# One load per input and chunk, the odd heads' halves exchanged in the results, and a new written order in an RWKV-6 and mixture-of-depths kernel

## The chip, the cores and the metric

The kernel runs on one core of a Trainium2 chip. The metric is the device time of one execution in microseconds (us): the median of 3 runs was 328.4 us (327.49 to 330.77). Everything is float32, except a few selection matrices in bfloat16.

## The reference, cut to what matters

First an RWKV-6 attention with B = 4 sequences, H = 8 heads, S = 768 steps, D = 48 columns a head. Each head carries a 48x48 state over the steps:

```
cur      = (u * k[t]) outer v[t]
y[t]     = r[t] @ (state + cur)
state    = w[t][:, None] * state + k[t] outer v[t]
```

The results are put side by side to x of shape (4, 768, 384). Then mixture of depths, with F = 1024 and capacity 128:

```
scores = x @ w_gate
for b: top = the 128 rows of x[b] with the highest scores
       out[b] = x[b];  out[b, top] += sigmoid(scores) * (relu(x[b, top] @ w1) @ w2)
```

## The kernel before, in words

The steps are cut into chunks of 128 (`L`), six to a sequence, so 24 chunks `n` in all; a chunk has two halves `q` of 64 steps. Within a chunk the recurrence is turned into matrix products: `logs` takes ln w, `sums` adds it up along the steps with a triangular matrix on TensorE, and `falling` (exp of minus the sum) and `rising` (exp of the sum without the own step, which `exclusive` makes) give the factors `e` by which `scaled` multiplies k and r. `turned` transposes the scaled k and r on TensorE, `keep` copies them out of PSUM, `scores` multiplies them, `masked` takes the part under the diagonal (the diagonal itself, with u, comes from `own_products`, `own_weighted`, `own_sums` and `own_diagonal`). `kv` makes k times v for each half, `middle`, `after` and `carried` keep the state, `from_state` and `from_chunk` add up y in the PSUM tile `ps_y`, `results` copies it out, `store` writes it to `out`, and `scored` multiplies it with w_gate.

Heads stand in pairs (even, odd) in one array of 128 rows; an odd head has its two halves exchanged in the rows. In the kernel before that exchange happens in the load: each input of a chunk comes in three transfers (`load`, L125 for the even heads, L127 twice for the halves of the odd ones), and tiles are kept by type of head. The factors lie with the four pairs innermost, a step of four elements. The decay over a chunk is fetched as two rows of `e` by two small transfers on ScalarE's queue (`decay_rows`) and inverted on VectorE (`decay`). `in_range` sums how far w lies under 0.7; `tick` issues it and orders two groups of TensorE writes behind each other. At the end a flag made from `guard` decides whether a general, slow path is run.

The mixture of depths follows per sequence b: `spread`, `spread_kept` and `compare` compare each score with all earlier ones, `column_sums`, `ranks`, `picks`, `numbers` and `index` make the list of rows, `fetch` gathers them from `out` by an indirect transfer on GpSimd's queue, `fetched_turned` and `fetched_kept` transpose them, eight `first` and eight `second` steps are the two products (`hidden` is the relu between them), `mixed` adds, `put` scatters the rows back. I call the 16 steps of one sequence its products.

The order in which steps are issued is written by hand: `at(turn, offset, step, n)` gives each step a place, the list is sorted by it, and each engine works through its instructions in that order. All loads and stores go through SyncE's queue (SP) in the same order. Inputs have 10 buffers, x has 4, the PSUM tile `ps_s` serves the sums, the scores and (as `ps_x`) everything of the mixture but the two products, which use `ps_m`.

Of the kernel before, what the change touches and what calls it, by code (L numbers as in the profile page):

```python
# [40 lines left out]
def kernel(  # L41
# [30 lines left out]
    assert B * NCH < 256  # L72
# [18 lines left out]
    def at(turn, offset, f, *args):  # L91
        plan.append((turn * TURN + offset, len(plan), f, args))
# [10 lines left out]
    def source(x, b, ci, t, q=None):  # L103
        lo, n = ci * L, L
        if q is not None:
            lo, n = ci * L + (1 - q) * Q, Q
        return by_type_h(x[b])[:, t, lo:lo + n, :].rearrange("j s d -> s j d")

    def by_type_h(x):
        return x.rearrange("(j t) s d -> j t s d", t=2)  # L110

    def load(n, which):
        if n >= N:
            return
# [10 lines left out]
        nc.sync.dma_start(out=dst[:, 0], in_=source(x, b, ci, 0))  # L125
        for q in (0, 1):
            nc.sync.dma_start(out=dst[q * Q:(q + 1) * Q, 1], in_=source(x, b, ci, 1, q))  # L127
# [4 lines left out]
    upper = consts.tile([L, 2, L], FP32)  # L132
# [5 lines left out]
    junk_1 = consts.tile([L, 1], FP32)  # L138
# [4 lines left out]
    u_bc = consts.tile([L, 2, HP, D], FP32)  # L143
# [53 lines left out]
    def load_w1(i):  # L197
        nc.sync.dma_start(out=w1[:, i], in_=w1_src[:, i])
# [8 lines left out]
    def flat(t):  # L207
        return t.rearrange("p t j d -> p (t j d)")

    def logs(n):  # L210
        lw = get(n, "lw", lev, [L, 2, HP, D], bufs=3)
        nc.scalar.activation(out=flat(lw), in_=flat(T[n, "w"]), func=AF.Ln)  # L212

    def in_range(n):
        junk = lev.tile([L, C], FP32, tag="junk", name="junk", bufs=1)
        return nc.scalar.activation(  # L216
            out=junk, in_=flat(T[n, "w"]), func=AF.Relu, bias=low, scale=-1.0,
            accum_out=guard[:, 0, n:n + 1],
        )

    def sums(n):
        for t in (0, 1):
            nc.tensor.matmul(  # L223
                ps_s[:, 0, t * HP * D:(t + 1) * HP * D], upper[:, t], T[n, "lw"][:, t],
                start=(t == 0), stop=True, skip_group_check=True,
            )

    summed = ps_s[:, 0, 0:C]

    def falling(n):  # L230
        e = get(n, "e", lev, [L, 2, 2, D, HP])
        nc.scalar.activation(  # L232
            out=e[:, 0].rearrange("p t d j -> p t j d"),
            in_=summed.rearrange("p (t j d) -> p t j d", t=2, j=HP), func=AF.Exp, scale=-1.0,
            accum_out=guard[:, 1, n:n + 1],
        )

    def exclusive(n):
        ex = get(n, "ex", lev, [L, 2, HP, D])
        nc.vector.tensor_sub(flat(ex), summed, flat(T[n, "lw"]))  # L240

    def rising(n):
        nc.scalar.activation(  # L243
            out=T[n, "e"][:, 1].rearrange("p t d j -> p t j d"), in_=T[n, "ex"], func=AF.Exp,
            accum_out=guard[:, 2, n:n + 1],
        )

    def decay_rows(n):
        if chunks[n][1] == NCH - 1:
            return  # L250
        for t in (0, 1):
            p = L - 1 if t == 0 else Q - 1
            nc.scalar.dma_start(
                out=a_rows[n % 3][t * DP:t * DP + D, :], in_=T[n, "e"][p:p + 1, 0, t],
            )

    def decay(n):
        if chunks[n][1] == NCH - 1:
            return
        a = get(n, "a", lev, [L, HP])  # L260
        nc.vector.reciprocal(out=a, in_=a_rows[n % 3])

    def scaled(n):
        nc.vector.tensor_mul(  # L264
            kr_t[n % 2][:, :, :, :, 0:D].rearrange("p j i t d -> p (i t) j d"),
            T[n, "kr"].rearrange("p i t j d -> p (i t) j d"),
            T[n, "e"].rearrange("p i t d j -> p (i t) j d"),
        )

    def turned(n, i):  # L270
        for j in range(HP):
            nc.tensor.transpose(  # L272
                ps_k[:, i, j * L:(j + 1) * L], kr_t[n % 2][:, j, i].rearrange("p t d -> p (t d)"), ident
            )
# [21 lines left out]

    halves = [slice(0, Q), slice(Q, L)]
# [11 lines left out]
    def masked(n):  # L309
        sc = T[n, "sc"].rearrange("p (t j) s -> p t (j s)", t=2)  # L310
        nc.vector.copy_predicated(  # L311
            out=T[n, "sc"].rearrange("p (t j) s -> p t j s", t=2),
            mask=_heads(within, 2, HP),
            data=ps_s[:, :, 0:HP * Q].rearrange("p t (j s) -> p t j s", j=HP),
        )

    def kv(n):
        ci = chunks[n][1]
        if ci == NCH - 1:
            qs = ((0, 0), (1, 1))  # L320
        else:
            qs = ((0, 0), (1, 0), (0, 1), (1, 1))
        for j in range(HP):
            for t, q in qs:
                half = q ^ t
                nc.tensor.matmul(
                    ps_k[halves[t], half, j * D:(j + 1) * D],
                    kr_t[n % 2][halves[q], j, 0, t, :], T[n, "v"][halves[q], t, j, :],
                    start=(j == 0), stop=True, skip_group_check=True,
                )  # L330
# [12 lines left out]
    def after(n):  # L343
# [3 lines left out]
        T[n, "sum"] = s  # L347
        nc.vector.tensor_add(s, kv_of(1), T[n, "mid"])

    def carried(n):  # L350
        if chunks[n][1] == NCH - 1:
            return
        nc.vector.tensor_mul(T[n, "sum"], T[n, "sum"], T[n, "a"].to_broadcast([L, HP, D]))

    def waits(later, first):
        tc.add_manual_dep(
            later.ins, first.ins.name,
            mybir.DependencyInfo(mybir.DependencyClass.Sync, mybir.DependencyReason.DATA),
            reason="other rows of the array write the same results",
        )  # L360

    def tick(n):

        if n + 4 < N:
            i = in_range(n + 4)
        else:
            i = nc.scalar.copy(out=junk_1, in_=low)
        if n >= 0:
            waits(i, T[n, "behind"])
            T[n, "tick"] = i  # L370

    def from_state(n):
        ci = chunks[n][1]
        for j in range(HP):
            for half in (0, 1):
                if half == 0 and ci == 0:
                    continue
                s = T[n, "mid"] if half else T[n, "state"]
                for t in (0, 1):
                    q = half ^ t  # L380
                    T[n, "behind"] = nc.tensor.matmul(  # L381
                        ps_y[halves[half], t, j * D:(j + 1) * D],
# [4 lines left out]
    def from_chunk(n):  # L387
        ci = chunks[n][1]
        sc = T[n, "sc"].rearrange("p (t j) s -> p t j s", t=2)
        for j in range(HP):  # L390
            for t in (0, 1):
                for q in (0, 1):
                    half = q ^ t
                    m = nc.tensor.matmul(  # L394
                        ps_y[halves[half], t, j * D:(j + 1) * D],
                        sc[halves[q], t, j, :], T[n, "v"][halves[q], t, j, :],
                        start=(ci == 0 and half == 0 and j == 0), stop=True, skip_group_check=True,
                    )
                    if j == 0 and t == 0 and q == 0:
# [364 lines left out]
```

## Time and profile before

| | |
|---|---|
| median of 3 runs | 328.4 us (327.49 to 330.77) |
| the profiled execution | 327.58 us, of which the profile's span is 325.8 us |
| busy: TensorE (PE), VectorE (DVE), ScalarE (ACT), GpSimd (POOL) | 194.3, 144.9, 120.5, 90.0 us |
| first and last `results` copy | 42.11 us and 293.29 us |
| mean granted TensorE clock | 0.781 |

A row of a list over time gives the start in us, the duration in us, the engine (PEld is the weight load of TensorE, SPq the SyncE queue), the line, the operation, output and input, and, in brackets, how long the engine was idle before it and what ended that. Grouped rows give the busy time in us and the mean of one in ns. A table by stretches gives the busy time of PE, PEld, DVE, ACT and POOL, then the granted clock, the busy share of the 16 DMA engines and GB/s. In the 40 slices of the span a digit is a tenth.

### The profile page before, as it was taken

The page shows a single profiled execution, that of the slowest core. Times are in us where ns is not written, and L with a number is a line of the kernel's source. Part 1 is how long each engine was busy: PE and PEld are TensorE (multiplying, and loading weights), DVE is VectorE, ACT ScalarE, POOL GpSimd, SP SyncE. Part 2 cuts the span into 40 slices and gives each one's busy share as a digit, 9 for nine tenths or more (in the row PEclk, how much of TensorE's full clock was granted, in tenths as well). Part 3 has the DMA queues.
Part 4 walks back from the last instruction along what each step waited for, and adds up shares of the span by engine and source line. Part 5 has one row for each costly group of instructions (what it writes and reads, how often), then busy time and mean ns, then how long its engine had stood idle before and what let it go on. Part 6 is the DMA issues. An engine that isn't in the chain of part 4 may idle for free.

```text
span 325.8 us, 8831 instructions
## 1 busy us (share of the span) xinstructions
PE 194.3 (60%) x3634; PEld 161.0 (49%) x3634; DVE 144.9 (44%) x356; ACT 120.5 (37%) x285; POOL 90.0 (28%) x94
## 2 busy tenths in 40 slices
PE   2033577766004668005797875788787798784890
PEld 1033466555003557005686653577665587662860
DVE  2125335554002674006555675466567576634100
ACT  2305444454002454001655542666555445330100
POOL 3131332134003140016134442333444612312001
PEclk9999955587555675555989995899999659998596
DMA  4575675666666656567555555640000200001001
GB/s 77 101 127 102 141 157 112 115 138 137 134 143 121 119 109 117 113 121 143 110 110 91 110 111 123 146 84 27 27 26 26 74 26 26 26 27 50 24 0 35
DMA packets 112208, 29.40 MB, mean 90 GB/s; under 512 B 107168, under 2 KB 111392, under 8 KB 112160
## 3 DMA queue, kind: packets, MB, share of 16 engines
q1 hardware_dynamic: 109088, 27.15, 40.9%
q0 software_dynamic: 512, 1.57, 1.6%
q8 instruction: 30, 0.49, 0.7%
q10 hardware_dynamic: 2560, 0.03, 0.4%
q14 instruction: 18, 0.15, 0.1%
HBM read 23.20 MB, written 5.51 MB: 88 GB/s over the span
## 4 chain that ended last, share of the span: by engine, by line
PE 25%; SPq 21%; issue 10%; DVE 9%; ACT 9%; DMA 7%; POOL 1%; ACTq 1%; DVEq 0%; POOLq 0%
SPq L127 14%; PE ps_k L272 7%; SPq L125 6%; PE ps_m L544 5%; ACT e L232 3%; PE ps_m L558 3%; PE ps_y L394 2%; PE ps_s L223 2%; DVE ex L240 2%; DMA out_dram<-x 2%; DVE scr L424 2%; DMA a_row<-e 2%; ACT x L409 1%; PE ps_y L381 1%; PE ps_s L303 1%
## 5 line engine op out<-in xcount | busy, mean ns | idle before, releaser
L295 POOL TENSOR_TENSOR sc<-diag,own 128x512 f32<-128x512 f32 x24 | 31.5, 1313 | 140.6 <-DVE own L289 127.5
L272 PE MATMUL ps_k<-ident,kr_t 128*128 128x128 f32 x192 | 36.9, 355 | 17.6 <-DVE kr_t L264 9.9
L264 DVE TENSOR_TENSOR kr_t<-kr,e 128x768 f32<-128x768 f32 x24 | 37.2, 1549 | 18.1 <-ACT e L243 11.0
L240 DVE TENSOR_TENSOR ex<-ps_s,lw 128x384 f32<-128x384 f32 x24 | 13.4, 558 | 65.8 <-ACT e L232 65.8
L272 PEld LDWEIGHTS ps_k<-ident,kr_t 128*128 128x128 f32 x192 | 29.6, 183 | 22.8 <-issue 12.5
L223 PE MATMUL ps_s<-lw,upper 128*128 128x192 f32 x96 | 28.1, 433 | 6.0 <-ACT lw L212 6.0
L544 PE MATMUL ps_m<-xeT,w 128*128 128x128 f32 x192 | 29.9, 312 | 2.3 <-ACT xeT L515 2.3
L394 PE MATMUL ps_y<-v,sc 64*64 64x48 f32 x768 | 19.7, 249 | 18.1 <-ACT junk L216 16.8
L424 DVE CUSTOM_DVE_ANT_0 scr<-x,wg_bc 128x384 f32<-128x384 f32 x24 | 13.5, 561 | 37.5 <-ACT x L409 37.4
L544 PEld LDWEIGHTS ps_m<-xeT,w 128*128 128x128 f32 x192 | 27.7, 222 | 4.0 <-ACT xeT L515 3.7
L435 PE MATMUL ps_s<-ident,score 128*128 128x128 f32 x24 | 8.7, 363 | 34.5 <-DVE score L424 34.1
L409 ACT COPY x<-ps_y 128x384 f32<-128x384 f32 x24 | 11.5, 478 | 46.1 <-PE ps_y L394 24.4
L285 POOL TENSOR_TENSOR rk<-rk,u_bc 128x384 f32<-128x384 f32 x24 | 24.3, 1012 | 13.4 <-DMA u_bc<-in_u_dram 11.6
L243 ACT ACTIVATE e<-ex 128x384 f32<-128x384 f32 x24 | 21.9, 913 | 15.1 <-DVE ex L240 15.1
L303 PE MATMUL ps_s<-RT,KT 64*64 64x64 f32 x768 | 19.7, 247 | 13.0 <-DVE ex L240 13.0
L216 ACT ACTIVATE junk<-w,low 128x384 f32<-128x384 f32 x24 | 14.7, 614 | 34.3 <-DMA w<-in_w_dram 22.0
L394 PEld LDWEIGHTS ps_y<-v,sc 64*64 64x64 f32 x768 | 17.2, 162 | 20.3 <-issue 19.2
L278 ACT COPY KT<-ps_k 128x512 f32<-128x512 f32 x24 | 14.0, 584 | 34.7 <-PE ps_k L272 34.7
L311 DVE COPY_PREDICATED sc<-within,ps_s 128x512 f32<-128x512 uint32 x24 | 17.4, 724 | 20.5 <-POOL sc L295 18.2
L282 POOL TENSOR_TENSOR rk<-kr 128x384 f32<-128x384 f32 x24 | 24.1, 1004 | 5.3 <-DMA kr<-in_r_dram 5.3
L558 PE MATMUL ps_m<-w,hid 128*128 128x384 f32 x64 | 25.4, 512 | 0.0
L223 PEld LDWEIGHTS ps_s<-lw,upper 128*128 128x128 f32 x96 | 22.3, 268 | 6.0 <-ACT lw L212 6.0
(87 smaller groups left out, 317.3 us busy)
## 6 DMA issues: line engine op xcount, KB each, us to landing
out_dram<-x SPq DMA_DIRECT2D x24, 192.0 KB, 2.1
w<-in_w_dram SPq DMA_DIRECT2D x24, 96.0 KB, 2.6
w<-in_w_dram SPq DMA_DIRECT2D x48, 48.0 KB, 2.8
kr<-in_k_dram SPq DMA_DIRECT2D x24, 96.0 KB, 2.8
kr<-in_k_dram SPq DMA_DIRECT2D x48, 48.0 KB, 2.4
kr<-in_r_dram SPq DMA_DIRECT2D x24, 96.0 KB, 2.6
kr<-in_r_dram SPq DMA_DIRECT2D x48, 48.0 KB, 2.4
v<-in_v_dram SPq DMA_DIRECT2D x24, 96.0 KB, 2.7
```

Of the source, the lines that this page charges most:

```text
L127: nc.sync.dma_start(out=dst[q * Q:(q + 1) * Q, 1], in_=source(x, b, ci, 1, q))
L223: nc.tensor.matmul(ps_s[:, 0, t * HP * D:(t + 1) * HP * D], upper[:, t], T[n, "lw"][:, t], start=(t == 0), stop=True, skip_group_check=True,)
L243: nc.scalar.activation(out=T[n, "e"][:, 1].rearrange("p t d j -> p t j d"), in_=T[n, "ex"], func=AF.Exp, accum_out=guard[:, 2, n:n + 1],)
L264: nc.vector.tensor_mul(kr_t[n % 2][:, :, :, :, 0:D].rearrange("p j i t d -> p (i t) j d"), T[n, "kr"].rearrange("p i t j d -> p (i t) j d" ...
L272: nc.tensor.transpose(ps_k[:, i, j * L:(j + 1) * L], kr_t[n % 2][:, j, i].rearrange("p t d -> p (t d)"), ident)
L282: nc.gpsimd.tensor_mul(flat(rk), flat(T[n, "kr"][:, 0]), flat(T[n, "kr"][:, 1]))
L285: nc.gpsimd.tensor_mul(flat(T[n, "rk"]), flat(T[n, "rk"]), flat(u_bc))
L295: nc.gpsimd.tensor_mul(sc, _heads(diag, H), T[n, "own"].to_broadcast([L, H, Q]))
L303: nc.tensor.matmul(ps_s[halves[q], t, j * Q:(j + 1) * Q], T[n, "KT"][halves[t], j, halves[q]], T[n, "RT"][halves[t], j, halves[q]], start= ...
L394: m = nc.tensor.matmul(ps_y[halves[half], t, j * D:(j + 1) * D], sc[halves[q], t, j, :], T[n, "v"][halves[q], t, j, :], start=(ci == 0 and ...
L544: nc.tensor.matmul(p[:, (f % GF) * L:(f % GF + 1) * L], w1[:, dc, f * L:(f + 1) * L], T[b, "xeT"][:, dc, :], start=(dc == 0), stop=(dc == ...
L558: nc.tensor.matmul(ps_m[0][:, 0:C], T[b, "hid"][:, f, :], w2[:, f, :], start=(f == 0), stop=(f == NFC - 1))
```

## The change

- **Loads.** One transfer for each input and chunk, all eight heads in their own order, 128 rows; w of two chunks lies in one tile `ww`. So 96 transfers where there were 288. u comes in one transfer instead of two, and w1 in four pieces instead of three.
- **Exchange.** The halves of odd heads are exchanged when `results` copies y out of PSUM: one copy for the even heads (128 rows) and two for the odd ones (64 rows each). `sums` is one product with one triangular matrix.
- **Unstrided factors.** `e` has the layout of k and r; `falling` and `rising` write densely and no longer accumulate into `guard`.
- **One decay row.** A third exponential on ScalarE (`whole`, 32 rows, written with a step of four) takes the place of the inverse; one transfer on SP's queue (`decay_row`) spreads its last row to 128 rows of `a_all`.
- **Range check.** `in_range` runs once for two chunks; `tick` and its waits go, `masked` waits for `from_state` of its chunk instead.
- **PSUM.** The sums have a bank of their own (`ps_x`), spread and counts lie in the free columns of `ps_s`, the two products use one bank `ps_m`, and for the last sequence `ps_s` and `ps_y`. x has 8 buffers, the small tiles of the mixture one for each sequence.
- **Order.** Each step has a place in a table instead of a hand-written offset, with a turn of 5.6 instead of 6.

```diff
 def load(n, which):
...
-    nc.sync.dma_start(out=dst[:, 0], in_=source(x, b, ci, 0))
-    for q in (0, 1):
-        nc.sync.dma_start(out=dst[q * Q:(q + 1) * Q, 1], in_=source(x, b, ci, 1, q))
+    nc.sync.dma_start(
+        out=dst.rearrange("p (h d) -> p h d", d=D),
+        in_=x[b, :, ci * L:(ci + 1) * L, :].rearrange("h s d -> s h d"),
+    )
...
 def sums(n):
-    for t in (0, 1):
-        nc.tensor.matmul(
-            ps_s[:, 0, t * HP * D:(t + 1) * HP * D], upper[:, t], T[n, "lw"][:, t],
-            start=(t == 0), stop=True, skip_group_check=True,
-        )
+    nc.tensor.matmul(summed, upper, T[n, "lw"], start=True, stop=True)
...
+def falling(n):
+    e = get(n, "e", lev, [L, 2, C])
+    nc.scalar.activation(out=e[:, 0], in_=summed, func=AF.Exp, scale=-1.0)
...
+def whole(n):
+    nc.scalar.activation(
+        out=falls[n % 2][:, :, 0:D, :].rearrange("p t d j -> p j t d"),
+        in_=summed[L - 32:L].rearrange("p (j t d) -> p j t d", t=2, d=D), func=AF.Exp,
+    )
+def decay_row(n):
+    nc.sync.dma_start(out=a_all[:, n, :], in_=falls[n % 2][31:32].rearrange("p t d j -> p (t d) j"))
 def scaled(n):
     nc.vector.tensor_mul(
-        kr_t[n % 2][:, :, :, :, 0:D].rearrange("p j i t d -> p (i t) j d"),
-        T[n, "kr"].rearrange("p i t j d -> p (i t) j d"),
-        T[n, "e"].rearrange("p i t d j -> p (i t) j d"),
+        kr_t[n % 2][:, :, :, 0:D].rearrange("p i h d -> p (i h) d"),
+        T[n, "kr"].rearrange("p i (h d) -> p (i h) d", d=D),
+        T[n, "e"].rearrange("p i (h d) -> p (i h) d", d=D),
     )
...
+def results(n, i):
+    if i == 0:
+        get(n, "x", lev, [L, H, D], bufs=8)
+    t, to, of = ((0, slice(0, L), slice(0, L)), (1, halves[0], halves[1]),
+                 (1, halves[1], halves[0]))[i]
+    nc.scalar.copy(
+        out=T[n, "x"].rearrange("p (j t) d -> p t j d", t=2)[to, t],
+        in_=ps_y[of, t, 0:HP * D].rearrange("p (j d) -> p j d", d=D),
+    )
...
+TURN = 5.6
+CHUNK_PLACES = {
+    "logs": -13.529, "in_range": 5.037, "sums": -10.782, "falling": -9.639, "exclusive":
+    -8.766, "rising": -7.796, "whole": -7.379, "decay_row": -1.446, "scaled": -6.003,
+    "own_products": -8.375, "own_weighted": -3.602, "own_sums": -3.578, "own_diagonal":
+    -0.431, "turned0": -5.178, "turned1": -4.856, "keep0": -3.586, "keep1": -3.296, "kv":
+    -2.911, "middle": -1.837, "after": -0.334, "carried": 3.13, "from_state": -0.146,
+    "scores": -1.822, "masked": 0.287, "from_chunk": 1.759, "results0": 2.506, "results1":
+    2.801, "results2": 3.124, "scored": 4.614, "store": 15.942, "spread": 5.503,
+    "spread_kept": 6.774, "compare": 6.875, "load_w": -17.786, "load_k": -13.524,
+    "load_r": -14.443, "load_v": -7.489,
+}
...
+BATCH_PLACES = {   # one place for each of the four sequences
...
+    "first0": (26.258, 30.275, 87.674, 215.849),
...
+    "second3": (51.842, 70.51, 224.53, 411.339),
...
+    "mixed": (61.705, 86.818, 305.931, 496.549),
```

Chunk n stands at 5.6 n plus its place, sequence b at 5.6 (6 b + 5) plus its place. Sorted, the order within a turn m is:

```
PE:   sums m+1, turned m, from_chunk m-1, kv m, scores m, from_state m, spread m-1, sums m+2
ACT:  keep m, results m-1 (three), logs m+2, rising m+1, whole m+1, in_range, spread_kept m-1, falling m+2
DVE:  exclusive m+1, carried m-1, middle m, scored m-1, scaled m+1, after m, masked m, compare m-1, own_sums m+1
SP:   decay_row m+1, load w m+4, store m-2, load r m+4, load k m+4, load v m+3
```

The stores of chunks 12 to 17 stand about one turn later than this.

More of the change, by code (lines that the diff above doesn't have):

```diff
@@ L22 @@
 LOW = 0.7
-LIMIT = 1.0e30
+LIMIT = 1.0e15
 NIN = 10
-TURN = 6.0
 def _rows(ap, n):
@@ L197, in load_w1 @@
     def load_w1(i):
-        nc.sync.dma_start(out=w1[:, i], in_=w1_src[:, i])
+        part = slice(i * F // 4, (i + 1) * F // 4)
+        nc.sync.dma_start(out=w1[:, :, part], in_=w1_src[:, :, part])
     def load_w2(i):
@@ L315, in masked @@
         )
-    def kv(n):
[L318 to L322, printed above, removed]
-        for j in range(HP):
[L324 to L330, printed above, removed]
+        tc.add_manual_dep(
+            i.ins, T[n, "behind"].ins.name,
+            mybir.DependencyInfo(mybir.DependencyClass.Sync, mybir.DependencyReason.DATA),
+            reason="other rows of the array write the same results behind this",
+        )
+    def kv(n):
+        last = chunks[n][1] == NCH - 1
+        for j in range(HP):
+            for q in (0,) if last else (0, 1):
+                for t in (0, 1):
+                    nc.tensor.matmul(
+                        ps_k[halves[t], q, j * D:(j + 1) * D],
+                        kr_t[n % 2][halves[q], 0, 2 * j + t, :], T[n, "v"][halves[q], 2 * j + t, :],
+                        start=(j == 0), stop=True, skip_group_check=True,
+                    )
     def kv_of(half):
@@ L352, in carried @@
             return
[L353 to L370, printed above, removed]
+        s = T[n + 1, "state"]
+        nc.vector.tensor_mul(s, s, a_all[:, n, :].to_broadcast([L, HP, D]))
     def from_state(n):
@@ L434, in spread @@
     def spread(b, c):
-        nc.tensor.transpose(ps_x[:, 0:L], score[:, b, c:c + 1].to_broadcast([L, L]), ident)
+        nc.tensor.transpose(ps_row, score[:, b, c:c + 1].to_broadcast([L, L]), ident)
     def spread_kept(b, c):
@@ L539, with bank @@
     GF = 4
+    def bank(b, g):
+        return (ps_s[:, g] if g < 2 else ps_y[:, 0]) if b == B - 1 else ps_m
     def first(b, f):
-        p = ps_m[(f // GF) % 2]
+        p = bank(b, f // GF)
         for dc in range(NDC):
@@ new lines, in in_range_even @@
+    def in_range_even(n):
+        if n % 2 == 1:
+            in_range(n - 1)
+    STEPS = dict(
+        logs=logs, in_range=in_range_even, sums=sums, falling=falling, exclusive=exclusive,
+        rising=rising, whole=whole, decay_row=decay_row, scaled=scaled, own_products=own_products,
+        own_weighted=own_weighted, own_sums=own_sums, own_diagonal=own_diagonal,
+        turned0=lambda n: turned(n, 0), turned1=lambda n: turned(n, 1),
+        keep0=lambda n: keep(n, 0), keep1=lambda n: keep(n, 1), kv=kv, middle=middle, after=after,
+        carried=carried, from_state=from_state, scores=scores, masked=masked,
+        from_chunk=from_chunk, results0=lambda n: results(n, 0), results1=lambda n: results(n, 1),
+        results2=lambda n: results(n, 2), scored=scored, store=store,
+        spread=lambda n: spread(*chunks[n]), spread_kept=lambda n: spread_kept(*chunks[n]),
+        compare=lambda n: compare(*chunks[n]), load_w=lambda n: load(n, "w"),
+        load_k=lambda n: load(n, "k"), load_r=lambda n: load(n, "r"), load_v=lambda n: load(n, "v"),
+    )
```

330 lines of the change are left out of this document (124 added, 206 removed), and 10 rows, old and new, of the table BATCH_PLACES.

## The prediction

> **What bounds the kernel now.** I read the page first: busy shares, slices, the chain of work that ended last.
>
> ```profile
> span 325.8 us, 8831 instructions
> PEclk9999955587555675555989995899999659998596
> DMA  4575675666666656567555555640000200001001
> q1 hardware_dynamic: 109088, 27.15, 40.9%
> PE 25%; SPq 21%; issue 10%; DVE 9%; ACT 9%; DMA 7%; POOL 1%; ACTq 1%; DVEq 0%; POOLq 0%
> SPq L127 14%; PE ps_k L272 7%; SPq L125 6%; PE ps_m L544 5%; ACT e L232 3%; PE ps_m L558 3%; PE ps_y L394 2%; PE ps_s L223 2%; DVE ex L240 2%; DMA out_dram<-x 2%; DVE scr L424 2%; DMA a_row<-e 2%; ACT x L409 1%; PE ps_y L381 1%; PE ps_s L303 1%
> ```
>
> No engine is busy all the time. The chain runs to 20% through the issue of loads on SP's queue (L127, L125), and the DMA engines are about 60% busy until slice 27 (some 215 us), then nearly idle. So there are two stages, and the queue's own list of instructions shows the first.
>
> ```profile
> 8.52 0.60 SPq L125 DMA_DIRECT2D w<-in_w_dram  x1
> 9.17 1.25 SPq L127 DMA_DIRECT2D w<-in_w_dram  x2
> 32.57 2.38 SPq L127 DMA_DIRECT2D v<-in_v_dram  x2
> 98.94 0.55 SPq L413 DMA_DIRECT2D out_dram<-x  x1
> 107.22 0.55 SPq L413 DMA_DIRECT2D out_dram<-x  x1
> 216.09 78.04 SPq L413 DMA_DIRECT2D out_dram<-x  x11
> ```
>
> One issue takes 0.60 us and 0.65 with its gap, for 96 KB (L125) as for 48 KB (L127: 1.25 for two). A chunk has twelve loads and a store, and the stores of neighbours stand 107.22 - 98.94 = 8.28 us apart: that is the queue's pace until 216 us. The first store waits behind ten chunks of loads until 98.94. What that does is seen in the copies of y out of PSUM (L409), one a chunk:
>
> ```profile
> 42.11 0.48 ACT L409 COPY x<-ps_y 128x384 f32<-128x384 f32 x1 [1.31 <-PE ps_y L394]
> 71.13 0.48 ACT L409 COPY x<-ps_y 128x384 f32<-128x384 f32 x1 [0.88 <-PE ps_y L394]
> 101.19 0.48 ACT L409 COPY x<-ps_y 128x384 f32<-128x384 f32 x1 [21.64 <-DMA out_dram<-x]
> 145.48 1.21 POOL L502 DMA_INDIRECT xe<-out_dram,idx  x1 [27.51 <-DMA w<-in_w_dram]
> 210.19 0.48 ACT L409 COPY x<-ps_y 128x384 f32<-128x384 f32 x1 [0.88 <-PE ps_y L394]
> 252.37 0.48 ACT L409 COPY x<-ps_y 128x384 f32<-128x384 f32 x1 [0.88 <-PE ps_y L394]
> 293.29 0.48 ACT L409 COPY x<-ps_y 128x384 f32<-128x384 f32 x1 [0.88 <-PE ps_y L394]
> ```
>
> Chunk 0 comes at 42.11. Chunk 4 waits 21.6 us for a buffer of x that the late store holds; the first gather (L502) waits 27.5 us, until the last store of its sequence has landed, also late in SP's queue. In the second stage nothing waits for loads, and still five chunks, 13 to 18, take 252.37 - 210.19 = 42.2 us, 8.4 each. So the time is 42.1 (head) + 251.2 (23 steps, two with a stall) + 32.5 (tail) = 325.8.
>
> **The change, part by part.** SP's queue: per chunk four loads, a store and the decay row, 6 x 0.65 = 3.9 us, if one issue of all eight heads costs what the two sizes seen cost. Twice the packets of L125 were never issued at once, so bounds: 0.6 (no dependence, which the equal rows say) to 1.95 us (the three it replaces). I take 0.65. The Trainium skill, Perfetto Trace Analysis, What "DMA-bound" means, reads a solid row of issues as the generation of descriptors, so the cost would grow with packets; the equal 0.60 speaks against it here, and a rival below carries it.
>
> The transfers themselves stay, packet for packet, but for the small decay rows. Queue q1 took 40.9% of 325.8 = 133 us of all 16 engines, 5.55 us a chunk with stores and weights. The fullest 5 us show what share they reach:
>
> ```profile
> 20.00:25.00 5.00, 0.77 (x3) 1.00 0.86 153
> 206.00:293.00 87.00, 69.86 (x1570) 58.13 (x1566) 54.98 (x138) 44.20 (x107) 30.59 (x28) 0.92 0.16 43
> 210.00:252.40 42.40, 34.12 (x770) 27.85 (x762) 28.54 (x69) 24.91 (x60) 16.95 (x15) 1.00 0.16 40
> ```
>
> At 0.86 a chunk takes 5.55 / 0.86 = **6.45 us** (at 1.0, 5.55).
>
> Engines: the third row holds five chunks, so 6.8 us of PE, 5.7 of DVE and 5.0 of ACT each. These rows carry the edits:
>
> ```profile
> L264 DVE TENSOR_TENSOR kr_t<-kr,e 128x768 f32<-128x768 f32 x24 | 37.2, 1549 | 18.1 <-ACT e L243 11.0 <-DMA kr<-in_k_dram 2.0 <-DMA kr<-in_r_dram 1.9
> L447 DVE SCALAR_TENSOR_TENSOR ahead<-every,score,ahead_of 128x768 bf16<-128x768 f32 x4 | 4.0, 1011 | 0.7 <-ACT every L440 0.7
> L232 ACT ACTIVATE e<-ps_s 128x384 f32<-128x384 f32 x24 | 21.0, 874 | 2.0 <-PE ps_s L223 1.9
> L243 ACT ACTIVATE e<-ex 128x384 f32<-128x384 f32 x24 | 21.9, 913 | 15.1 <-DVE ex L240 15.1
> L212 ACT ACTIVATE lw<-w 128x384 f32<-128x384 f32 x24 | 12.6, 523 | 0.0
> L409 ACT COPY x<-ps_y 128x384 f32<-128x384 f32 x24 | 11.5, 478 | 46.1 <-PE ps_y L394 24.4 <-DMA out_dram<-x 21.6
> L440 ACT COPY every<-ps_s 128x128 f32<-128x128 f32 x24 | 6.4, 265 | 19.0 <-PE ps_s L435 18.7
> L278 ACT COPY KT<-ps_k 128x512 f32<-128x512 f32 x24 | 14.0, 584 | 34.7 <-PE ps_k L272 34.7
> ```
>
> - `scaled` on dense factors: between nothing gained (1.55) and the other fp32 operation of 768 elements (1.01). I take 1.0: DVE about 5.1 us a chunk, without the inverse less still.
> - `falling` and `rising`, dense and without reading an accumulator: as `logs`, 0.52 each, where 0.87 and 0.91 stood (at worst these). `whole` has the strided row's 0.87. `results`: three copies of 192 elements, between 0.265 (128) and 0.478 (384), so about 0.33 each, 1.0 in all for 0.48. The range check halves its fixed part. ACT stays near 5 us a chunk.
>
> PE loses the second triangular product's instructions; POOL does what it did. Now the loop. In the sorted order `turned` of a chunk stands behind `sums` of the next but one (they share `ps_x` with `whole`), so at full clock:
>
> ```profile
> 171.58 1.09 PE L272 MATMUL ps_k<-ident,kr_t 128*128 128x128 f32 x8 [0.34 <-DVE state L348]
> 172.51 0.82 PE L223 MATMUL ps_s<-lw,upper 128*128 128x192 f32 x4
> 43.91 1.97 PE L272 MATMUL ps_k<-ident,kr_t 128*128 128x128 f32 x8 [0.19 <-DVE state L348]
> 42.10:62.50 20.40, 15.65 (x282) 13.28 (x282) 10.26 (x24) 9.44 (x22) 6.14 (x6) 0.50 0.64 138
> ```
>
> `turned` 1.09, two `keep` 1.17, three `results` 1.0, `logs` 0.52, `rising` 0.52, `whole` 0.87, `sums` about 0.7, less some 0.1 of overlap at each of five ACT neighbours: 5.4 us around. A new wait in it is `sums` behind `whole`, and behind `sums` all of PE is queued; the other, `masked` behind `from_state`, ends well before DVE gets there. The decay row's wait holds SP's next loads, but those are wanted a turn or more later. So per turn: SP 3.9, loop 5.4, DVE 5.1, DMA 6.45. PE: 25 of the 64 product steps stand in the main loop, the rest behind it, about 0.7 us each:
>
> ```profile
> 214.27 1.34 PE ps_m L544 x12
> 298.56 3.18 DMA xe<-out_dram,idx
> 303.31 8.39 PE ps_m L544 x48
> 311.70 5.18 PE ps_m L558 x16
> 317.87 0.99 POOL out_dram L570
> ```
>
> (x12 are two `first` steps in 1.34; x16 are eight `second` in 5.18.) The stretch of five chunks held about one sequence's 16 steps, 10.6 us, so a bare chunk is (34.1 - 10.6) / 5 = 4.7, and the new main loop has 4.7 + 25 x 0.67 / 23 = 5.4. The transfers end last: I take **6.5 us** a turn.
>
> Head: `results` of chunk 0 stands behind `turned` of chunk 1, which needs w of chunk 2 by way of ACT's order. Ahead of that load SP has ten, 2.2 MB with one piece of w1; at 153 GB/s of the fullest window 14 us, plus 3 to issue and land, one load more (1.3), then `logs`, `rising`, `scaled`, `turned` and `from_chunk`, 4 us: **22**. Bounds 19 (larger packets move faster) and 27.
>
> Tail, from the last `results`: half of the products stand here. On PE five `second` of sequence 1 (3.2), all of sequence 2 and of sequence 3 (2 x 10.6), and some 6 for turns, counts and the one bank that sequence 2 has: 30.5; the gather's 3.2 us lie beside sequence 2. Behind PE come `mixed`, `put` and the end, 325.8 - 316.9 = 8.9 as before (PE ended at 311.70 + 5.18). **39**, against 32.5.
>
> Sum: 22 + 23 x 6.5 + 39 = 210.5; the profiled execution lay 1.8 over its span (327.58) and the median another 0.8 over that: **213 us**.
>
> **The rivals.**
>
> 1. *Engines bound, transfers fill up to 1.0.* 20 + 23 x 5.6 + 39 + 2 = 190. For it: 5.55 us of transfers fit. Against: no window is over 0.86.
> 2. *The pace stays.* Engines in order wait for each other as in chunks 13 to 18 (8.4), or the DMA share stays at 0.64 (5.55 / 0.64 = 8.7): 22 + 23 x 8.5 + 39 + 2 = 258. For it: both were measured. Against: the 8.4 had the strided operations and a decay row on ACT's queue inside the loop, and 0.64 went with a queue that issued no faster.
> 3. *The change's loads do not get cheaper to issue* (the skill's reading): 1.95 each, 4 x 1.95 + 1.2 = 9.0 a turn: 270.
> 4. *TensorE stays at half clock.* In 42.1 to 62.5 PE was busy 7.8 us a chunk at 0.50; `turned` took 1.97 for 1.09. With the products 1.3 more, 9.1 a turn, and 17 more in the tail: 289. For it: the slices show it at half for long stretches, 40 to 65 us among them. Against: with PE at 80% it was 1.00 for 42 us. The Trainium skill, TensorE: Matmul & The Clock Gate, PE-mode transpose, says that transposes don't count as activity; by it this loop, a quarter of which transposes, would be more apt to fall, but the 1.00 stretch had the same share.
> 5. *Slower: SP's queue chokes on large loads.* Now and then an issue takes 1.1 us longer (32.57: 2.38 for two instead of 1.25). If that is a queue that is full, a load of twice the largest size would meet it twice, 0.6 + 2.2 = 2.8: a turn of 4 x 2.8 + 1.2 = 12.4, 348 in all. It turns slower than before from about 2.6 us an issue. Against: that stall is rare and follows no size.
>
> **How the numbers follow.** Forecast 0.55 (its own range 203 to 232: half a us a turn either way, the head's bounds, some turns at half clock), rival 1 0.12, rival 2 0.19, rival 3 0.06, rival 4 0.05, rival 5 0.03. The range 188 to 264 leaves out rivals 3 to 5 and the edges of the first two, about 0.2. Faster by over 1% (about what a measurement here can tell from no change) are all but the last: 0.96; within 1% 0.01; slower 0.03.
>
> **What would show it.** First `results` near 22 us, 23 steps of 6.5 without one of 20, the last near 171. A DMA share over 0.8 until about 150 us; loads of 0.6 us on SP; `scaled` at 1.0, `falling` and `rising` at 0.5, `whole` at 0.9; products of two sequences behind the last chunk. I am wrong if a turn takes 8 us with the DMA share under 0.7 (the order, not the transfers), if SP is solid, if PE's clock is 0.5 in the main loop, or if the tail is over 45.

## The result, and the profile after

The changed kernel takes 221.6 us (219.12 to 222.56, 4 runs) where the kernel before took 328.1 beside it (327.49 to 330.77): a ratio of 0.672 [0.665, 0.679]. The forecast was 213. The profiled execution took 221.88 us, 220.0 of them in the span. First the page, as it was read before:

```profile
span 220.0 us, 8419 instructions
PEclk9999999999988999999999979999999999999995
DMA  6999797878979795795978683568841221010002
q1 hardware_dynamic: 109728, 27.19, 59.1%
DVE 32%; PE 26%; ACT 19%; issue 9%; DMA 7%; SPq 4%; POOL 0%; POOLq 0%; DVEq 0%; ACTq 0%
```

SP's queue has gone from the chain (21% to 4%), the clock no longer falls to half, and 27.19 MB (27.15 before) now take 59.1% of a shorter span, 130 us. VectorE leads the chain. The copies of y give the three parts of the time (ScalarE's rows, first and last of 24):

```profile
22.14 0.99 ACT L361 COPY x<-ps_y 128x192 f32<-128x192 f32 x3
182.02 0.97 ACT L361 COPY x<-ps_y 128x192 f32<-128x192 f32 x3 [0.50 <-PE ps_y L349]
```

Head 22.1, 23 steps in 159.9 us (6.95 each), tail 220.0 - 182.0 = 38.0. Before it was 42.1, 251.2 (10.9 each) and 32.5. So the head gave 20 us, the steps 91, and the tail took back 5.5. The table by stretches shows the main loop in thirds and as a whole, with the fullest five us ahead (busy us of PE, PEld, DVE, ACT, POOL, then clock, DMA share, GB/s):

```profile
15.00:20.00 5.00, 4.15 (x82) 3.37 (x83) 2.91 (x5) 2.50 (x5) 1.99 (x3) 1.00 1.10 194
22.10:69.30 47.20, 35.77 (x962) 26.87 (x962) 41.91 (x80) 32.65 (x77) 23.96 (x22) 0.96 0.82 176
69.30:124.50 55.20, 48.83 (x1178) 37.23 (x1178) 50.69 (x100) 39.70 (x94) 26.78 (x24) 1.00 0.80 170
124.50:182.00 57.50, 46.82 (x1141) 36.03 (x1140) 48.69 (x94) 35.45 (x85) 26.37 (x24) 0.97 0.53 116
22.10:182.00 159.90, 131.42 (x3279) 100.13 (x3280) 141.28 (x272) 107.79 (x253) 77.10 (x69) 0.98 0.71 152
```

A share of 1.10 was reached, so neither 0.86 nor 1.0 was a ceiling of this figure, and in the last third, where the share is 0.53, the turn is no shorter. VectorE is busy 141.28 of 159.9 us, 6.14 a turn, where I had counted 5.1. The groups of instructions show which of its operations grew (busy us, then the mean of one in ns):

```profile
L241 DVE TENSOR_TENSOR kr_t<-kr,e 128x768 f32<-128x768 f32 x24 | 32.7, 1362 | 1.1 <-ACT e L228 1.1
L379 DVE CUSTOM_DVE_ANT_0 scr<-x,wg_bc 128x384 f32<-128x384 f32 x24 | 23.2, 968 | 0.7 <-ACT x L361 0.6
L328 DVE TENSOR_TENSOR state<-state,a_all 128x192 f32<-128x192 f32 x20 | 18.7, 933 | 0.0
L222 ACT ACTIVATE e<-ps_x 128x384 f32<-128x384 f32 x24 | 11.9, 497 | 6.2 <-PE ps_x L218 6.2
L232 ACT ACTIVATE fall<-ps_x 32x384 f32<-32x384 f32 x24 | 20.9, 869 | 0.6
L361 ACT COPY x<-ps_y 64x192 f32<-64x192 f32 (+1 forms) x72 | 23.4, 325 | 2.3 <-PE ps_y L349 1.6
```

ScalarE's durations are those forecast. On VectorE `scaled` (L241), `scored` (L379) and `carried` (L328) are not: 192 elements took 0.93 us. The two engines' lists beside each other show why:

```profile
144.96 0.95 DVE L241 TENSOR_TENSOR kr_t<-kr,e 128x768 f32<-128x768 f32 x1
148.88 1.05 POOL L273 TENSOR_TENSOR sc<-diag,own 128x512 f32<-128x512 f32 x1 [4.27 <-DVE own L267]
149.12 1.02 DVE L328 TENSOR_TENSOR state<-state,a_all 128x192 f32<-128x192 f32 x1
149.88 1.12 POOL L263 TENSOR_TENSOR rk<-rk,u_bc 128x384 f32<-128x384 f32 x1
150.96 1.31 POOL L260 TENSOR_TENSOR rk<-kr 128x384 f32<-128x384 f32 x1
151.35 1.74 DVE L241 TENSOR_TENSOR kr_t<-kr,e 128x768 f32<-128x768 f32 x1
```

GpSimd's three steps of a chunk run in a row behind `own_sums`. `carried`, begun beside the first, ends at 150.14, just behind that one's end (149.93). `scaled`, begun beside the third, takes 1.74 and ends 0.8 behind its end; at 144.96, with GpSimd idle, it takes 0.95. In the whole run the 10 `scaled` that meet no step of GpSimd take 0.95 or 0.96, the 14 that begin beside one 1.66 on average. So theory **A**: a VectorE instruction with two operands in SBUF waits for the GpSimd instruction that is at work, and these waits make the turn. The Trainium skill, SBUF — State Buffer, Who interferes with whom, has the rule: "A DVE instruction with two SBUF inputs contends with a GpSimd instruction that reads SBUF". The durations agree with it; whether the turn hangs on it is another question. The list of waits shows a way by which it could (us in total, times, longest): `turned` (L249) writes the PSUM tile that `after` (L322) reads, and `after` stands behind `scaled` in VectorE's order.

```profile
PEld ps_k L249 <- DVE state L322: 15.7, 18, 1.6
```

Rivals: **B**, the transfers hold the turn, as I had forecast; **C**, something else does, the engines' written order above all.

### The profile page after: what moved, and what is told of

It reads as the page before. It is cut to its first block, busy times and chain, and to the rows that moved or that the text cites. A ratio compares the mean times of both kernels' runs of the same rounds, so it can differ in the third digit from the quotient of the medians.

```text
span 220.0 us, 8419 instructions
## 1 busy us (share of the span) xinstructions
PE 169.9 (77%) x3586; PEld 127.8 (58%) x3586; DVE 159.7 (73%) x332; ACT 122.3 (56%) x281; POOL 91.3 (42%) x94
## 3 DMA queue, kind: packets, MB, share of 16 engines
q1 hardware_dynamic: 109728, 27.19, 59.1%
## 4 chain that ended last, share of the span: by engine, by line
DVE 32%; PE 26%; ACT 19%; issue 9%; DMA 7%; SPq 4%; POOL 0%; POOLq 0%; DVEq 0%; ACTq 0%
DVE scr L379 6%; DVE kr_t L241 6%; DVE sc L286 5%; ACT x L361 5%; PE ps_m L506 4%; PE ps_m L520 4%; PE ps_k L249 3%; DMA ww<-in_w_dram 3%; DVE state L328 3%; PE ps_x L218 3%; ACT lw L206 3%; PE ps_s L506 3%; ACT fall L232 2%; PE ps_y L520 2%; SPq L120 2%
## 5 line engine op out<-in xcount | busy, mean ns | idle before, releaser
L249 PEld LDWEIGHTS ps_k<-ident,kr_t 128*128 128x128 f32 x192 | 23.5, 151 | 20.7 <-DVE state L322 15.7
L249 PE MATMUL ps_k<-ident,kr_t 128*128 128x128 f32 x192 | 28.2, 293 | 7.2 <-DVE state L322 5.7
L241 DVE TENSOR_TENSOR kr_t<-kr,e 128x768 f32<-128x768 f32 x24 | 32.7, 1362 | 1.1 <-ACT e L228 1.1
L218 PE MATMUL ps_x<-lw,upper 128*128 128x384 f32 x48 | 24.2, 590 | 11.2 <-ACT lw L206 7.0
L361 ACT COPY x<-ps_y 64x192 f32<-64x192 f32 (+1 forms) x72 | 23.4, 325 | 2.3 <-PE ps_y L349 1.6
L379 DVE CUSTOM_DVE_ANT_0 scr<-x,wg_bc 128x384 f32<-128x384 f32 x24 | 23.2, 968 | 0.7 <-ACT x L361 0.6
L302 PE MATMUL ps_k<-v,kr_t 64*64 64x48 f32 x704 | 16.7, 226 | 7.3 <-ACT RT L256 7.3
L402 DVE SCALAR_TENSOR_TENSOR ahead<-every,score,ahead_of 128x128 bf16<-128x128 f32 (+5 forms) x24 | 16.4, 684 | 7.3 <-ACT every L395 7.2
L232 ACT ACTIVATE fall<-ps_x 32x384 f32<-32x384 f32 x24 | 20.9, 869 | 0.6
L302 PEld LDWEIGHTS ps_k<-v,kr_t 64*64 64x64 f32 x704 | 13.7, 138 | 11.2 <-ACT RT L256 10.5
L338 PE MATMUL ps_y<-mid,RT 64*64 64x48 f32 x384 | 17.1, 225 | 2.3 <-DVE mid L314 0.7
L328 DVE TENSOR_TENSOR state<-state,a_all 128x192 f32<-128x192 f32 x20 | 18.7, 933 | 0.0
L506 PEld LDWEIGHTS ps_m<-xeT,w 128*128 128x128 f32 x144 | 17.3, 191 | 2.1 <-ACT xeT L473 0.9
L225 DVE TENSOR_TENSOR ex<-ps_x,lw 128x384 f32<-128x384 f32 x24 | 13.2, 548 | 6.5 <-ACT e L222 6.5
```

The costliest lines, as they stand in the source:

```text
L218: nc.tensor.matmul(summed, upper, T[n, "lw"], start=True, stop=True)
L232: nc.scalar.activation(out=falls[n % 2][:, :, 0:D, :].rearrange("p t d j -> p j t d"), in_=summed[L - 32:L].rearrange("p (j t d) -> p j t ...
L241: nc.vector.tensor_mul(kr_t[n % 2][:, :, :, 0:D].rearrange("p i h d -> p (i h) d"), T[n, "kr"].rearrange("p i (h d) -> p (i h) d", d=D), T ...
L249: nc.tensor.transpose(ps_k[:, i, j * L:(j + 1) * L], kr_t[n % 2][:, i, 2 * j:2 * j + 2].rearrange("p t d -> p (t d)"), ident,)
L302: nc.tensor.matmul(ps_k[halves[t], q, j * D:(j + 1) * D], kr_t[n % 2][halves[q], 0, 2 * j + t, :], T[n, "v"][halves[q], 2 * j + t, :], sta ...
L361: nc.scalar.copy(out=T[n, "x"].rearrange("p (j t) d -> p t j d", t=2)[to, t], in_=ps_y[of, t, 0:HP * D].rearrange("p (j d) -> p j d", d=D),)
```

## The experiments

**Do the transfers hold the turn?** `e2_no_v_loads` leaves out the loads of v from chunk 2 on, a quarter of all loads (later chunks use the v of chunk 0 or 1).

```diff
         elif which == "v":
+            if n >= 2:
+                T[n, "v"] = T[n % 2, "v"]
+                return
```

> Leaves out the loads of v but for the first two chunks (the others use those), a quarter of the load traffic. Theory A, VectorE waits for GpSimd: within 1% of 221, the DMA share falls from 0.82 to about 0.65 in the first seven turns. Theory B, the transfers hold the turn: a turn of about 5.6 instead of 6.95, 190 in all. Theory C, the loop: 221.

Measured: 219.7 us, ratio 0.669 [0.663, 0.674]; the stretch of the first chunks:

```profile
22.10:69.30 47.20, 35.48 (x978) 26.59 (x974) 42.12 (x80) 32.62 (x77) 23.75 (x21) 0.96 0.67 148
```

The DMA share falls from 0.82 to 0.67 and the time stays. B falls, and with it the term on which my sum stood. The same edit thins out SP's issues: from 25 to 50 us they fill 62% of the time, where they fill 95% in the changed kernel; so the queue does not hold the turn either.

**Do GpSimd's products cost VectorE time?** `e1_no_pool_products` leaves out `own_products` and `own_weighted` from chunk 2 on (`own_sums` then works on old data); `own_diagonal` stays.

```diff
 def own_products(n):
+    if n >= 2:
+        T[n, "rk"] = T[n % 2, "rk"]
+        return
 def own_weighted(n):
+    if n >= 2:
+        return
```

> Leaves out GpSimd's two products of k, r and u for all chunks but the first two (the diagonal then uses those of chunks 0 and 1). Theory A, VectorE waits for GpSimd: with GpSimd down from 3.4 to 1.04 us a turn, carried falls from 0.93 to 0.36, scored from 0.97 to 0.57, scaled from 1.36 to 1.0, that is 1.3 us less of VectorE a turn; the turn goes from 6.95 to about 6.2, where the transfers or TensorE hold it, and the time from 221 to about 204. Theory B, the transfers hold the turn: 220 to 222. Theory C, the loop through ScalarE and TensorE holds it: 220 to 222 as well.

Measured: 203.6 us, ratio 0.620 [0.614, 0.626]. Its groups, and its middle third:

```profile
L241 DVE TENSOR_TENSOR kr_t<-kr,e 128x768 f32<-128x768 f32 x24 | 23.0, 958 | 2.5 <-ACT e L228 2.2
L384 DVE CUSTOM_DVE_ANT_0 scr<-x,wg_bc 128x384 f32<-128x384 f32 x24 | 13.5, 561 | 1.1 <-ACT x L366 1.0
L333 DVE TENSOR_TENSOR state<-state,a_all 128x192 f32<-128x192 f32 x20 | 19.2, 960 | 0.0
69.30:124.50 55.20, 51.94 (x1201) 40.86 (x1192) 44.63 (x102) 42.55 (x97) 10.47 (x10) 0.97 0.90 189
```

`scaled` and `scored` fall to 0.96 and 0.56; `carried`, which still meets `own_diagonal`, stays at 0.96. TensorE is now busy 51.94 of 55.2 us, 94%, which makes it the likely next bound. The edit also takes work from GpSimd itself (77.1 us in the main loop fall to 27.2), so this run alone does not tell VectorE's waits from GpSimd's own time. `e3_neither` is both edits at once, to see whether the transfers (share 0.90) take over there.

> Leaves out own_products and own_weighted and, from chunk 2 on, the loads of v. Without the two products alone it was 203.6 us with a DMA share of 0.90. If the transfers hold that turn of 6.2 (my forecast's limit, one step later), a quarter less of loads gives 5.4-5.6: 186-192 us. If VectorE, waiting for own_diagonal, or the loop holds it: 200-204 us.

Measured: 204.2 us, ratio 0.625 [0.621, 0.629], the same as `e1`. The transfers are not even the second limit.

**What was the gain of the large loads worth?** `e4_three_loads` issues each load in three pieces, as the kernel before did, into the same tile.

```diff
-        nc.sync.dma_start(out=dst..., in_=x[b, :, ci * L:(ci + 1) * L, :]...)
+        for rows, heads in ((slice(0, L), 0), (slice(0, Q), 1), (slice(Q, L), 1)):
+            nc.sync.dma_start(out=dst...[rows, :, heads], in_=...[heads, part])
```

> Undoes one part: each load is issued as three again (even heads, two halves of the odd heads), to the same places, nothing else changed. If the issue on SP's queue was what bound the kernel before, a turn takes 12 x 0.65 + 2 x 0.6 = 9.0 us until the last load: 22 + 6 (head) + 23 x 9.0 + 38 = 273. If the gain of the change came from the order and the engines, 221 to 230.

Measured: 289.2 us, ratio 0.877 [0.868, 0.886]. SP's rows, here and, in the second fence, in the changed kernel:

```profile
64.79 0.56 SPq L240 DMA_DIRECT2D a_all<-fall  x1
72.89 1.91 SPq L122 DMA_DIRECT2D v<-in_v_dram  x3
74.89 0.56 SPq L240 DMA_DIRECT2D a_all<-fall  x1
```

```profile
72.73 0.58 SPq L120 DMA_DIRECT2D ww<-in_w_dram  x1
74.04 0.37 SPq L120 DMA_DIRECT2D kr<-in_r_dram  x1
74.46 0.70 SPq L120 DMA_DIRECT2D kr<-in_k_dram  x1
75.26 1.22 SPq L120 DMA_DIRECT2D v<-in_v_dram  x1
```

Three issues take 1.91 us. One of the same bytes takes 0.59 for w, 0.58 for r and 0.70 for k (medians of 24), but 1.01 for v, which stands last of the four, and up to 2.89. With three, SP's turn is 74.89 - 64.79 = 10.1 us and solid. So 68 of the 107 us come back with the number of issues and what follows from it (the mean granted clock falls from 0.972 to 0.825). By the rule of the Trainium skill that the prediction weighed (Perfetto Trace Analysis, What "DMA-bound" means) the single large issue, with the same packets, should have kept the price of its descriptors. For w, r and k it didn't, for v half of it stayed.

**What were the dense factors worth?** `e8_strided` writes the factors with the head innermost again.

```diff
-        nc.scalar.activation(out=e[:, 0], in_=summed, func=AF.Exp, scale=-1.0)
+        nc.scalar.activation(out=e[:, 0].rearrange("p (d h) -> p h d", h=H), in_=by_head(summed), ...)
...
-            T[n, "e"].rearrange("p i (h d) -> p (i h) d", d=D),
+            T[n, "e"].rearrange("p i (d h) -> p i h d", h=H),
```

> Undoes the dense factors alone (the head is innermost in e, a step of eight elements; the kernel before had four). scaled rises by about 0.6 us (1.55 for 0.96), falling and rising by 0.35-0.4 each. If VectorE's order sets the turn, +0.6 a turn: 23 x 0.6 = 14, 232-238 us; if rising is on the loop too, +1.0 a turn: 242-248. If the transfers or GpSimd set it: 220-224 us.

Measured: 238.2 us, ratio 0.726 [0.722, 0.730], 16.5 over the changed kernel or 0.7 a turn. That lies at the edge of the case of VectorE's order. But `scaled` rose by 0.45 us only, from 1.36 to 1.81, so it does not make up the turn alone; `falling` and `rising` rose by 0.39 each (to 0.88 and 0.90), and their part was not separated.

**Does the turn hang on VectorE's waits?** Four kernels take waits away without taking work away. `e5_carried_early` issues `carried` right behind `after`, where GpSimd is idle.

```diff
-        "carried": 3.13,
+        "carried": -0.333,
```

> Moves carried right behind after in the written order, away from own_diagonal on GpSimd, which starts 0.2 us ahead of it now; nothing else changed. Theory A, VectorE waits for GpSimd: carried falls from 0.93 to 0.36, up to 0.57 x 20 = 11 us less, 210 to 216, if the next operation with two inputs in SBUF does not wait in its place. Theories B and C: 220 to 222.

Measured: 224.3 us, ratio 0.683 [0.677, 0.689].

```profile
L241 DVE TENSOR_TENSOR kr_t<-kr,e 128x768 f32<-128x768 f32 x24 | 39.8, 1657 | 1.4 <-ACT e L228 1.3
L328 DVE TENSOR_TENSOR state<-state,a_all 128x192 f32<-128x192 f32 x20 | 7.9, 394 | 0.8
PEld ps_k L249 <- DVE state L322: 21.1, 19, 2.7
```

`carried` falls from 0.93 to 0.39 us and `scaled` rises from 1.36 to 1.66: the wait has moved to the next instruction with two SBUF operands. Behind `scaled` stands `after`, and `turned` now waits 21.1 us for it, where it was 15.7.

`e7_both_in_psum` leaves the order and moves one operand of each: `after` writes the state to free columns of `ps_s`, and the weights of the gate are copied once into free columns of `ps_y`.

```diff
-        nc.vector.tensor_add(s, kv_of(1), T[n, "mid"])
+        nc.vector.tensor_add(ps_state, kv_of(1), T[n, "mid"])
...
-        nc.vector.tensor_mul(s, s, a_all[:, n, :].to_broadcast([L, HP, D]))
+        nc.vector.tensor_mul(s, ps_state, a_all[:, n, :].to_broadcast([L, HP, D]))
```

> Same steps and order; the state before its decay and the weights of the gate are kept in PSUM, so that carried and scored read one operand from SBUF instead of two. A (a VectorE instruction with two SBUF operands waits for a GpSimd one that is at work): carried falls from 0.93 to 0.35-0.45 us, scored from 0.97 to 0.55-0.65; scaled, the next one with two SBUF operands, now starts about 1.9 us behind own_sums, while GpSimd still has about 1.2 us to run, so it rises to 1.6-2.0 and gives part back: a turn of 6.3-6.6 for 6.95, 206-214 us. B (their length comes from the broadcast operand or from the memory of the result, whatever GpSimd does): both stay at 0.9-1.0, 220-223 us.

Measured: 225.0 us, ratio 0.686 [0.682, 0.690]. Its groups, and its list of waits (us in total, times, longest):

```profile
L246 DVE TENSOR_TENSOR kr_t<-kr,e 128x768 f32<-128x768 f32 x24 | 31.4, 1310 | 3.3 <-ACT e L233 3.0 <-issue 0.2
L379 DVE CUSTOM_DVE_ANT_1 scr<-x,ps_y 128x384 f32<-128x384 f32 x24 | 13.1, 545 | 1.4 <-ACT x L365 1.3
L332 DVE TENSOR_TENSOR state<-ps_s,a_all 128x192 f32<-128x192 f32 x20 | 7.0, 348 | 1.0 <-PE ps_s L444 1.0
PE ps_s L397 <- DVE ps_s L326: 14.1, 16, 2.3
PE ps_y L342 <- DVE score L379: 7.9, 11, 2.0
```

This settles the mechanism: same instruction, same place, same GpSimd work beside it, and 0.93 becomes 0.35, 0.97 becomes 0.55 when one operand lies in PSUM; `scaled`, which keeps two in SBUF, still takes 1.31. But the time does not fall. TensorE got two waits that the changed kernel hasn't: `spread` (L397) for `after`, which now writes to the same tile, and `from_state` (L342) for `scored`, which now reads from that of y. Behind `spread` stand `sums` and `turned`.

`e10_psum_own_early` adds to it that `own_sums` and GpSimd's three steps stand ahead of `after`, beside instructions with one SBUF operand.

```diff
-  "own_products": -8.375, "own_weighted": -3.602, "own_sums": -3.578, "own_diagonal": -0.431
+  "own_products": -11.4, "own_weighted": -11.3, "own_sums": -5.95, "own_diagonal": -5.9
```

> As the kernel with both operands in PSUM, and own_sums moved ahead of after in VectorE's order, with the three GpSimd steps right behind it. A: GpSimd's 3.1 us now lie beside after, masked, exclusive, carried, middle and scored, which read at most one operand from SBUF; only compare collides. scaled falls to 0.95-1.1 us and a turn to 5.6-6.1: 195-207 us. Rival: own_products now stands only 2 places behind the load of k (5 before), GpSimd waits for the load and VectorE for GpSimd: 215-230 us. B (no collision at all): 220-223 us.

Measured: median 226.9 us (223.2 to 227.2).

```profile
L246 DVE TENSOR_TENSOR kr_t<-kr,e 128x768 f32<-128x768 f32 x24 | 23.0, 957 | 3.4 <-ACT e L233 3.2
```

All three waits are gone (`carried` 0.34, `scored` 0.55), and the time is what it was. Taken alone that would have refuted A for the turn. But TensorE's two waits that came with the operands in PSUM are still there, 16.1 us in `spread` and 6.9 in `from_state`. So the waits had to be removed without an operand in PSUM. `e11_regrouped` only changes places: `carried`, then `own_sums` and GpSimd's steps, right behind `after`.

```diff
+  "carried": -0.333, "own_sums": -5.932, "own_diagonal": -5.93, "own_products": -11.4, "own_weighted": -11.3
```

> Only places in the order differ: carried right behind after, own_sums right behind it, and the three GpSimd steps behind own_sums; no operand in another memory, so none of the new waits of TensorE for VectorE that the two kernels with operands in PSUM had. GpSimd's 3.1 us then begin about 0.9 us behind the end of after, beside masked, exclusive and middle, which read one operand from SBUF. A (VectorE's waits for GpSimd stand in the loop after, turned, keep, results, logs, rising, scaled, after): carried 0.35-0.4, scaled 0.96-1.1, scored and compare still collide now and then; a turn of 6.0-6.4, 203-212 us. B (the turn is held by something else, the waits only fill VectorE's idle time, as the 225 us with the operands in PSUM would say): 219-225 us.

Measured: 225.6 us, ratio 0.686 [0.681, 0.691], just over the 219 to 225 that the text on record gives for B. But the copies of y of chunks 10 and 15 say otherwise, first of the changed kernel, then of this one, then one row of this one's waits:

```profile
88.69 1.02 ACT L361 COPY x<-ps_y 128x192 f32<-128x192 f32 x3
124.47 0.99 ACT L361 COPY x<-ps_y 128x192 f32<-128x192 f32 x3
```

```profile
94.31 0.99 ACT L361 COPY x<-ps_y 128x192 f32<-128x192 f32 x3
127.39 0.99 ACT L361 COPY x<-ps_y 128x192 f32<-128x192 f32 x3
PE ps_m L469 <- DMA xe<-out_dram,idx: 11.8, 2, 6.0
```

Five steps take 35.8 us there and 33.1 here, 7.16 against 6.62 a turn. That is a favourable stretch: over all steps but the two with the waits of the last row, 21 of 23, it is 6.80 against 6.60. So the turn did get shorter, and the wait of `turned` for `after` is down from 15.7 us to 0.6. The gain went to two waits of 6 us: TensorE reaches `fetched_turned` (L469) before the gathered rows have landed, and everything in order behind it stands still. `e14_gather_early` issues the gather ahead of `own_diagonal` in GpSimd's queue and places `fetched_turned` and what follows about a turn later.

```diff
-  "fetch": (22.157, 27.695, 33.685, ...), "fetched_turned": (23.291, 28.434, ...)
+  "fetch": (19.5, 24.5, 28.8, ...), "fetched_turned": (27.95, 33.5, ...)
```

> As the regrouped order (225.6 us), and for sequences 0 and 1 the gather stands ahead of own_diagonal in GpSimd's queue instead of behind it (for sequence 2 earlier too), and fetched_turned with what follows about one turn later in TensorE's order. In the regrouped kernel TensorE stood 11.8 us in two waits for the gathered rows, and all in-order work behind it. If the gain of the freed VectorE was given back there, the two waits go and the time is 211-216 us, under the 221.6 of the changed kernel; a turn stays at 6.1-6.4. If the turn itself was not made shorter by the regrouping and the two waits only took the place of idle time, 220-226 us.

Measured: **213.8 us** (212.4 to 216.6), ratio 0.649 [0.645, 0.653], 11.9 less than `e11` and below the changed kernel with intervals apart. The first and last `results` stand at 22.54 and 174.44, so a turn is 6.60 over the whole loop, where it was 6.95. The waits for the gather are gone. The changed kernel's list has no such wait, so the earlier gather had none to remove there; it was not tried without the regrouping. The wait of `turned` for `after`, and the two longest waits left to TensorE in the loop:

```profile
PEld ps_k L249 <- DVE state L322: 1.0, 3, 0.6
PE ps_k L302 <- ACT RT L256: 11.2, 14, 1.2
PE ps_x L218 <- ACT fall L232: 8.2, 12, 2.8
```

`kv` (L302) waits for `keep`, 11.2 us (7.3 in the changed kernel), and `sums` for `whole`, 8.2 (4.0), the wait that the prediction had named in its loop. `e15_logs_late` asks which of two ways holds the turn now, by moving `logs` behind `rising`.

```diff
-        "logs": -13.529
+        "logs": -13.25
```

> As the one before, and logs moved from ahead of rising to behind it on ScalarE, so that rising, scaled and after come 0.5 us earlier. If the turn is held by the way turned, keep, results, logs, rising, scaled, after, turned: a turn 0.2-0.5 us shorter, 201-210 us. If it is held by the way turned, keep, results, logs, rising, whole, sums, turned (sums writes the bank that whole reads, and stands ahead of turned), or by TensorE, nothing changes: within 2 us of the one before.

Measured: 211.7 us (209.8 to 213.2), ratio 0.643 [0.639, 0.647]. That is 2.1 less, with intervals that overlap: `scaled` does not hold the turn alone any more; whether `whole` and `sums` do or TensorE, which is busy 83% of the loop, these runs don't separate. It is the fastest version that computes everything.

`e12_compare_late` took `compare` out of GpSimd's way too, on the order of `e11`.

```diff
-  "compare": 6.875
+  "compare": 10.3      (and the sums over it as much later)
```

> As the one before, and compare moved from before exclusive to behind scored, where GpSimd has almost ended. A: compare no longer meets GpSimd, exclusive comes 0.7-1.0 us earlier; scored takes over a part of the wait. 0-0.3 us a turn better than the kernel before: 198-210 us. If compare now delays scaled, which stands behind it and in the loop, it is 0.3-0.7 a turn worse: 212-224 us. B: 219-225 us.

Measured: 234.5 us, ratio 0.712 [0.707, 0.717].

```profile
L402 DVE SCALAR_TENSOR_TENSOR ahead<-every,score,ahead_of 128x128 bf16<-128x128 f32 (+5 forms) x24 | 16.2, 680 | 0.0
DVE ex L225 <- ACT e L222: 19.4, 22, 4.1
```

`compare` is 0.68, where it was 0.79 in `e11`, but `exclusive` only changed one wait for another (19.4 us for `falling`), and `compare` now stands between `scored` and `scaled`. The two waits for the gather are in this kernel too (11.3 us in all), so it is to be held against `e11`, which it exceeds by 8.8. It is slower than the rival's own 212 to 224; what makes up the rest was not taken apart.

## Why the prediction was right in its number and wrong in its reason

The number is right by luck: the transfers' 6.45 us a turn and the turn that VectorE's waits make lie near each other, and the head came out for a reason that is not the one given.

- **Head**: 22 forecast, 22.1 measured, but not as reckoned. The sum let the load of w of chunk 2 end last, 18.3 us in. The `logs` of chunks 1 and 2 show otherwise:

```profile
9.46 0.52 ACT L206 ACTIVATE lw<-ww 128x384 f32<-128x384 f32 x1 [0.32 <-DMA ww<-in_w_dram]
15.69 0.54 ACT L206 ACTIVATE lw<-ww 128x384 f32<-128x384 f32 x1
```

  Chunk 2 starts at 15.69 and waits for no load; from the load that ends at 9.46 on, the engines' order makes the head. With the same loads and another order it is 20.3 (`e5`).
- **Tail**: 39 forecast, 38.0 measured. TensorE ends 30.4 us behind the last `results`, as reckoned (30.5); 7.5 stand behind it, for 8.9.
- **The turn**: 6.5 forecast, 6.95 measured; 23 x 0.45 = 10.4 us too little, less the 0.9 that head and tail had too much: that is the 9.5 by which the span of 220.0 exceeds 210.5. The step that failed is "the transfers end last". Its 6.45 came from the fullest window of a profile whose queue could not issue faster; the share reached 1.10 as soon as it could, and a quarter less of loads changed nothing (`e2`, `e3`). "A DMA share over 0.8 until about 150 us" held, at 0.82 and 0.80, until 124.5 and was then 0.53.
- **The term that was mis-sized is VectorE's**: 5.1 forecast, 6.14 measured. I took its operations at their mean durations before and did not ask what GpSimd would be doing beside them. By `e1` and `e7` the waits are (1.36 - 0.96) + (0.97 - 0.56) + (0.93 - 0.35) = 1.4 us for a chunk; in `e14`, without most of them, VectorE is busy 116.4 us of the loop, 5.1 a turn, as forecast.
- **The loop left VectorE out**: it went from `keep` by way of ScalarE to `sums`, and its sum has no `scaled` and no `after`, which `turned` waited for 18 times. (In it `turned` stands behind `sums` of the next chunk, not of the next but one; the sum is the same.) Freed of VectorE's waits, a turn is 0.35 shorter (`e14`), most of the 0.45 by which the forecast was short; `e1`, which also takes work from GpSimd, makes it 0.72 shorter.
- **Rival 1** (the engines are the bound) had the right kind of answer and the wrong size, 5.6 a turn, for the same reason. `e1`, which has fewer collisions, comes nearest to it.
- **SP**: 0.65 an issue forecast; 0.58 to 0.70 measured for w, r and k, and 1.01 for v (medians), so that the four loads of a chunk took 3.5 us on average, for 2.6. "SP is solid", which the prediction named as a sign of being wrong, was nearly so from 25 to 50 us (95%), but `e2` shows that it did not set the turn: neither rival 3 nor rival 5. No wait for a store is left on ScalarE. `e4` gives 68 us of the 107 to this step, `e8` 16.5 to the dense factors. The order and the larger buffers were not tried alone, and such parts need not add up.
- **Durations**: `scaled` 1.0 (0.96 alone, 1.36 with the waits), `falling` 0.52 (0.50), `whole` 0.87 (0.87), `results` 0.33 (0.325); the clock was 0.97. These hold, `scaled` but for the waits.

## What to carry to other kernels

When a bottleneck goes, the next one is to be read from what runs beside what, not from mean durations: here a VectorE instruction with two operands in SBUF took longer as soon as an order put it beside one of GpSimd's. Take a busy share reached behind a bottleneck as a measurement of that bottleneck, not as a ceiling. And an order written by hand is tuned as a whole: a faster turn gave nothing until the gather was issued earlier too.

## What the runs showed of the hardware

Beside a GpSimd instruction VectorE's `carried` took 0.93 us on average with both operands in SBUF and 0.35 with one in PSUM; where `e5` had no GpSimd instruction beside it, it took 0.36 with both in SBUF. Issuing 192 KB in 1024 packets took SP 0.58 to 0.70 us at the median for w, r and k, about what 48 KB took before (0.60), but 1.01 for v. The granted clock was 0.98 in the main loop, where TensorE was busy 82% of the time, and 0.67 from 42 to 206 us of the kernel before, where it was busy 56%; both loops hold the transposes.
